# A contiguous copy of each position's spectrum ahead of its matmuls, and one pipeline of four stages for all rows

## The chip, the cores and the metric

The kernel runs on one core of one Trainium2 chip. The metric is the time of one execution in device microseconds, as the median of several runs. All data is float32 (or float32r, a one-pass float32 matmul form, where the code says F32R).

## What is computed

A gate mixes two branches over the same input `x` (2048 tokens, 640 features):

```python
def _A_ref(x, wqkv, wo):          # 32 heads of 20, each token sees itself and 7 others, 2 apart
    ...
    logits = jnp.einsum("bhsd,bhswd->bhsw", q, kg) * scale
    ...
    attn = _softmax(logits, axis=-1)
    o = jnp.einsum("bhsw,bhswd->bhsd", attn, vg)
    return (lambda x, *d: x.transpose(*d))(o, 0, 2, 1, 3).reshape(B, S, D) @ wo

def _B_ref(x, w_r, w_i):          # a filter in the two-dimensional spectrum
    X = jnp.fft.rfft2(x, axes=(-2, -1))
    X = X * (w_r + 1j * w_i)
    return jnp.fft.irfft2(X, s=(S, D), axes=(-2, -1))

x = A_x
g = _sigmoid((x * gate_w).sum(-1, keepdims=True))
return g * _A_ref(x, A_wqkv, A_wo) + (1 - g) * _B_ref(x, B_w_r, B_w_i)
```

## The kernel before, in words

**Tiling.** Token number 16p + j stands in partition p at position j, so there are 128 partitions and `NJ` = 16 positions. The transform over the 2048 tokens is one of length 128 over the partitions (matmuls with the table `fc`) followed by a step of length 16 over the positions. The spectrum lies in one SBUF tile `zg` of shape [128, 5, 16, 8, 16]: the partition is one of 128 feature frequencies, then come 5 chunks t of feature frequencies, 16 groups g of row frequencies, 8 entries c of a group, and last the position j. For a fixed chunk and group, the 128 numbers (c, j) lie side by side. For a fixed chunk and position, the 128 numbers (g, c) lie 16 numbers, 64 bytes, apart.

**Stages.** (1) `qkv`: the projection in three F32R matmuls per product (high and low halves), written to DRAM and read back by `attend`, which runs 16 units of attention mostly on DVE and POOL. (2) `cols`: the transform over the partitions, written by ACT into `zg` with a step of 64 bytes (`zg<-z`). (3) `freq(g)` (lines 919 to 1021), for 16 groups: matmuls with `zg[:, t, g]` as the stationary operand (`u`, `v`), the step over positions, the filter on DVE and POOL, and the way back over features of the group, copied by ACT into `zg` again (`zg<-g`, two copies for a group, chunks 0 to 2 and 3 to 4). (4) `project_even(j)`: the output projection for even positions, ending in a transfer to DRAM (`ad`). (5) `spatial(j)` (lines 1039 to 1109), the way back over rows for one position: six matmuls with the 128 numbers `zg[:, t, :, :, j]` as the stationary operand give `oa` and `ob`; ACT copies them to `os`; four matmuls with `fct` give `ha` and `hb`; for an odd position ACT scales these to `ho` and stops there, for an even one ACT and DVE make the row `y` (six DVE instructions, `h`, `ha`, `y`) and POOL adds it to what `project_even` left, by a transfer that accumulates (`yi<-y`, positions 0 to 8) or an addition. (6) `project_odd(j)` (lines 1140 to 1174): POOL folds `ho` into `ye` and `y`, PE projects the odd positions (`oTp`, `woa`, `wob`), DVE adds.

A matmul in float32 stands in the trace as two instructions, each with its own load of weights (PEld); one in F32R stands as one.

**Order.** `Plan` records every operation, with the buffers it reads and writes, and a planner (lines 286 to 481) then decides the order on each engine from its own costs and a seeded search over 250 variations; each engine runs its list strictly in that order. All instructions therefore carry line 666, and the tile names tell them apart. A buffer that two names share (a tag of a ring) must be used in the order in which the program names its users. `staged(gens, n)` names the steps of several generators so that n of them are under way at once.

**Tags and banks that matter here.** `oa` and `ob` turn over PSUM banks 0 to 2, `ha` over 3 and 4, `hb` has 5; `project_odd` takes banks 0 to 4 in turn for `woa`, `wob`, so the `wob` of its second position stands in bank 3. `ev0` and `ev1` hold the tables `mm` of `freq` until its last group; `x6` holds products of `freq` (line 573) and then `ye` of `project_odd` (line 577). The rows `y` turn over `raw3`, `raw4`, `e0` and `ya` (line 578).

Of the kernel before, what the change touches and what calls it, by code (L numbers as in the profile page):

```python
# [17 lines left out]
NJ = 16  # L18
# [487 lines left out]
def staged(gens, n):  # L506
    for step in range(len(gens) + n - 1):
        for i in range(max(0, step - n + 1), min(step, len(gens) - 1) + 1):
            next(gens[i], None)


class Ring:
# [5 lines left out]
    def next(self, name, *shape, dtype=F32):  # L518
        self.turn += 1
        tag = self.tags[(self.turn - 1) % len(self.tags)]  # L520
        return self.pool.tile([128, *shape], dtype, tag=tag, name=name, bufs=1)


class Mixer:
# [17 lines left out]
    def places(self, pp, dr, sb):  # L542
        self.pp, self.sb = pp, sb
        qb = self.pp.tile([128, 512], F32, tag="qbank", name="qbank")
        self.qthird = [qb[:, GC * i : GC * i + GC] for i in range(3)]
        self.qturn = -1
        self.qkv_d = dr.tile([8, 6, ROWS, HC], F32, tag="dram_qkv", name="qkvd")
        self.o_d = [dr.tile([128, 8, D], F32, tag=f"dram_o{i}", name=f"od{i}") for i in range(2)]
        self.f_d = dr.tile([128, 8, 2, D], F32, tag="dram_f", name="fd")
        self.a_d = dr.tile([128, 8, D], F32, tag="dram_a", name="ad")  # L550
        self.ident, self.fc = (self.one(n, 128) for n in ("ident", "fc"))
        self.fct = self.one("fct", 2, 128)
        self.z, self.g, self.ng, self.nng = (self.one(n, NJ) for n in ("z", "g", "ng", "nng"))
        make_identity(self.nc, self.ident)
        self.low = self.one("low", 64)
        self.nc.gpsimd.memset(self.low, -1e9)

        def ring(*tags):
            return Ring(sb, *tags)

        def n(tag, k):
            return ring(*(f"{tag}{i}" for i in range(k)))


        self.kvr, self.Lr, self.qr, self.prr = n("kv", 6), n("L", 3), n("q", 2), n("pr", 2)
        self.mr, self.sr, self.orr, self.pvr = n("m", 2), n("s", 2), n("o", 2), n("pv", 2)

        self.xr, self.wr, self.evr, self.rawr, self.fr = n("x", 8), ring(*WPLACES), n("ev", 2), n("raw", 5), n("f", 2)
        self.er, self.xor = ring("fe0", "fe1"), ring("raw0", "raw1", "raw2", "raw3", "raw4", "kv4", "kv5", "ya")

        self.vsr, self.mdr, self.mfr, self.wpr = n("raw", 2), n("ev", 2), ring("mf"), n("f", 2)
        self.abr, self.Pr, self.s12r, self.Xr = ring("x0", "x1"), ring("x2", "x3"), ring("x4", "x5"), ring("raw3", "raw4")
        self.p1r = ring("x6", "raw2")

        self.wor, self.war, self.yar = ring("ya", "w7"), ring("w2", "w3", "w4", "w0", "w1", "w5", "w6"), ring("ya")
        self.otr, self.oTr = (ring("w7"), ring("w7", "kv2")), (ring("x7"), ring("x7", "pr0"))
        self.osr, self.hor, self.hyr, self.yer = n("raw", 3), n("x", 4), ring("x4", "x5"), ring("x6")
        self.yr, self.yir = ring("raw3", "raw4", "e0", "ya"), n("f", 2)
        self.banks = {}
# [9 lines left out]
    def work(self):  # L589
        p, ins = self.p, self.ins  # L590
        S = p.sp
        self.xT, self.wh, self.wl, self.folded = {}, {}, {}, {}
        self.xraw, self.wraw = {}, {}
        self.warm()
        xe = self.one("xe", 8, 2, 5, 128, dtype=F32R, tag="big")
        st = [t[:, i] for t in (self.xr.next(f"st{i}", 2, 641) for i in range(7)) for i in range(2)]
        p.rank = 1e6
        self.load_x(st, xe[:, 0], 0)
        self.load_w(st, 0)
        for j in range(2, NJ, 2):  # L600
            self.load_x(st, xe[:, j // 2], j)
        self.xr.turn = 0
        self.fold(0)
        self.fold(1)
        rank, p.rank = p.rank, 0.0
        S.dma_start(self.fc, ins["t_fc"][:, 0:128])
        self.zero_rows()
        self.qkv(0, 0)
        p.rank = rank
        for j in range(1, NJ, 2):  # L610
            self.load_x(None, self.xr.next(f"xo{j}", 2, 5, 128, dtype=F32R), j)
        p.rank = 0.0
        for q in STORED:
            self.fold(q)
        self.qkv(1, 0)
        for hg in (1, 2, 3):
            self.load_w(None, hg)
            self.qkv(0, hg)
            if hg == 1:
                self.qkv(1, hg)  # L620
        self.zg = self.one("zg", 5, 16, 8, NJ, tag="big")
        todo = list(range(8))

        def columns(jj):
            if jj % 2:
                q = todo.pop(0)
                self.cols(q)
                if q + 2 in STORED:
                    self.load_f(q + 2)
                elif q < 6:  # L630
                    self.fold(q + 2)

        self.qkv(1, 2, columns)
        self.qkv(1, 3, columns)
        self.bt, self.gt = self.one("bt", 1288, tag="e0"), self.one("gt", 1288, tag="e1")
        S.dma_start(self.bt[:, 0:1284], ins["t_bt"])
        S.dma_start(self.gt, ins["t_gt"])
        S.dma_start(self.fct.rearrange("p v m -> p (v m)"), ins["t_fc"][:, 128:384])
        self.gates()
        self.load_wo()  # L640
        for u in UNITS[:-2]:
            staged([self.attend(*u)], 3)
        pair = [self.attend(*u, 2) for u in UNITS[-2:]]
        for _ in range(5):
            for a in pair:
                next(a, None)
        p.chain = ""
        freq = [self.freq(g) for g in GORD]
        staged(freq, 4)
        p.chain = "even"  # L650
        for j in range(0, NJ, 2):
            self.project_even(j)
        p.chain = ""
        staged([self.spatial(j) for j in range(1, NJ, 2)], 2)
        staged([self.spatial(j) for j in range(0, NJ, 2)], 3)
        odd = [self.project_odd(j) for j in range(1, NJ, 2)]
        next(odd[0])
        for this, later in zip(odd, odd[1:] + [iter(())]):
            next(later, None)
            next(this, None)  # L660
# [378 lines left out]
    def spatial(self, j):  # L1039
        p = self.p  # L1040
        V, A, T = p.dve, p.act, p.pe
        zg, gt = self.zg, self.gt
        o1, o2 = (self.ps((0, 1, 2), f"o{i}{j}") for i in "ab")

        def mm(o, t, r, start, stop):
            T.matmul(o, zg[:, t, :, :, j].rearrange("p g c -> p (g c)"), r, start=start, stop=stop, skip_group_check=True)

        mm(o1[:, 0:322], 1, gt[:, 161:483], True, False)
        mm(o1[:, 0:161], 0, gt[:, 0:161], False, False)
        mm(o1[:, 161:322], 2, gt[:, 483:644], False, True)  # L1050
        mm(o2[:, 0:322], 3, gt[:, 805:1127], True, False)
        mm(o2[:, 0:161], 2, gt[:, 644:805], False, False)
# [7 lines left out]
        for i, h in enumerate((h1, h2)):  # L1060
            for a in range(2):
# [4 lines left out]
                    start=(a == 0),  # L1066
                    stop=(a == 1),
                    skip_group_check=True,
# [182 lines left out]
```

## Time and profile before

| | |
|---|---|
| median of 3 runs (lowest, highest) | 465.19 us (464.69, 466.1) |
| the profiled execution: its own time, and the span of its trace | 464.31 us, 462.5 us |
| granted TensorE clock in it | 0.999 |
| busy shares over the span | PE 98%, PEld 87%, DVE 85%, ACT 48%, POOL 73% |

PE is a matmul, PEld a load of weights, which can run beside a matmul; DVE, ACT and POOL are the vector, scalar and GpSimd engines, SP issues most transfers. A row of instructions gives start, duration, engine, line, operation, `out<-in`, and in brackets the idle time just ahead of it with what ended that time. The ends of matmuls are modelled, so a busy PE is not PE at its peak. In this trace `freq` ends, and `spatial` begins, near 340 us; the last `ha` of `spatial` starts near 418 us, and what follows is `project_odd`.

### The profile page before, as it was taken

Reading aid. Unit: us, or ns where it says so; the run is one execution under the profiler, and the core shown is the slowest. Engines: PE = TensorE matmul, PEld = TensorE weight load, DVE = VectorE, ACT = ScalarE, POOL = GpSimd, SP = SyncE. Lnnn points to the kernel's source line nnn. Section 1 sums busy time; section 2 is a strip of 40 time slices with the busy share of each in tenths; the row PEclk is TensorE's granted clock in tenths of the full one; section 3 lists DMA queues with packets and bytes.
Section 4 is the critical chain, followed back from the end, with each engine's and each line's share of the span. In section 5 each row is a group of like instructions: output and inputs, shape, how many; then the busy total and the mean of one; then the engine's idle time right before and its main releaser. Section 6 shows DMA issues by size and latency. Waiting matters only on the chain.

```text
span 462.5 us, 7087 instructions
## 1 busy us (share of the span) xinstructions
PE 454.7 (98%) x2437; PEld 404.6 (87%) x2437; DVE 394.9 (85%) x515; ACT 221.2 (48%) x546; POOL 339.9 (73%) x296
## 2 busy tenths in 40 slices
PE   8999999999999999999999999999999999999996
PEld 5888888888888889898888878988889999999996
DVE  4545799999999999999999989999997897969443
ACT  5464364233332234565578587676745444332110
POOL 1075066879999998997599997355867966856796
PEclk9999999999999999999999999999999999999999
DMA  8995989585657749899797758866433132676842
GB/s 303 373 312 161 374 256 350 165 244 154 206 158 224 220 119 330 260 308 285 211 356 218 216 194 229 289 213 187 142 101 95 44 96 73 178 208 177 250 171 85
DMA packets 87283, 98.65 MB, mean 213 GB/s; under 512 B 20416, under 2 KB 74816, under 8 KB 87248
## 3 DMA queue, kind: packets, MB, share of 16 engines
q1 hardware_dynamic: 47616, 63.64, 43.9%
q10 hardware_dynamic: 38864, 32.86, 22.6%
q0 software_dynamic: 768, 1.71, 2.0%
q8 instruction: 19, 0.31, 0.3%
q14 instruction: 16, 0.13, 0.1%
HBM read 66.33 MB, written 30.22 MB: 209 GB/s over the span
## 4 chain that ended last, share of the span: by engine, by line
PE 78%; issue 7%; DVE 5%; DMA 5%; POOL 3%; ACT 2%; ACTq 0%; POOLq 0%; DVEq 0%
PE qkv L666 33%; PE woa L666 7%; PE wob L666 6%; PE oa L666 5%; PE ob L666 5%; PE z L666 4%; PE v L666 3%; PE g L666 3%; PE u L666 3%; PE hb L666 2%; PE ha L666 2%; DMA xt<-in_xT 2%; PE oTp L666 2%; POOL xo L666 2%; PE xa L666 2%
## 5 line engine op out<-in xcount | busy, mean ns | idle before, releaser
L666 PE MATMUL qkv<-w,xo 128*128 128x480 f32 (+1 forms) x480 | 114.0, 386 | 0.0
L666 PE MATMUL qkv<-w,xe 128*128 128x480 f32 (+1 forms) x465 | 105.4, 382 | 0.2 <-POOL w L666 0.2
L666 PEld LDWEIGHTS qkv<-w,xo 128*128 128x128 f32 x480 | 89.4, 189 | 13.4
L666 PEld LDWEIGHTS qkv<-w,xe 128*128 128x128 f32 x465 | 87.5, 189 | 15.4 <-POOL w L666 0.6
L666 ACT COPY ev<-qkv 128x480 f32<-128x480 f32 x64 | 35.7, 559 | 50.1 <-PE qkv L666 38.8
L666 PE MATMUL woa<-wo,oT 128*128 128x320 f32 x240 | 49.2, 316 | 0.1
L666 PE MATMUL wob<-wo,oT 128*128 128x320 f32 x240 | 48.4, 313 | 0.0
L666 PEld LDWEIGHTS woa<-wo,oT 128*128 128x128 f32 x240 | 38.4, 188 | 0.7 <-ACT oT L666 0.3
L666 PEld LDWEIGHTS wob<-wo,oT 128*128 128x128 f32 x240 | 38.5, 188 | 0.0
L666 POOL TENSOR_TENSOR P<-X,wp 128x642 f32<-128x642 f32 x16 | 24.9, 1556 | 18.3 <-ACT X L666 17.3
L666 POOL TENSOR_TENSOR w<-raw,w 128x480 fp32r<-128x480 f32 x15 | 18.2, 1239 | 19.5 <-ACT w L666 19.5
L666 POOL TENSOR_TENSOR xo<-xt,xo 128x640 fp32r<-128x640 f32 x8 | 12.4, 1580 | 22.2 <-ACT xo L666 20.0
L666 PE MATMUL oa<-gt,zg 128*128 128x161 f32 (+1 forms) x96 | 28.0, 408 | 0.6 <-ACT zg L666 0.6
L666 ACT CAST oT<-oTp 128x384 fp32r<-128x384 f32 (+1 forms) x32 | 13.0, 427 | 28.6 <-PE oTp L666 23.8
L666 PE MATMUL ob<-gt,zg 128*128 128x161 f32 (+1 forms) x96 | 26.6, 402 | 0.0
L666 DVE TENSOR_TENSOR oT<-oTp,oT 128x384 fp32r<-128x384 f32 (+1 forms) x32 | 15.0, 485 | 12.9 <-ACT oT L666 12.9
L666 PEld LDWEIGHTS g<-mm,s 128*128 128x128 f32 x150 | 20.9, 191 | 4.3 <-ACT zg L666 2.0
L666 PEld LDWEIGHTS oa<-gt,zg 128*128 128x128 f32 x96 | 23.8, 305 | 0.8 <-ACT zg L666 0.8
L666 PEld LDWEIGHTS ob<-gt,zg 128*128 128x128 f32 x96 | 24.1, 305 | 0.0
L666 ACT COPY zg<-z 128x512 f32<-128x512 f32 (+1 forms) x24 | 20.7, 948 | 6.4 <-PE z L666 6.4
L666 PE MATMUL g<-mm,s 128*128 128x128 f32 x150 | 22.8, 277 | 0.3 <-ACT zg L666 0.3
L666 PE MATMUL u<-bt,zg 128*128 128x321 f32 (+2 forms) x96 | 22.4, 345 | 0.0
(304 smaller groups left out, 1087.5 us busy)
## 6 DMA issues: line engine op xcount, KB each, us to landing
qkvd<-ev ACTq DMA_DIRECT2D x32, 480.0 KB, 4.1
wp<-in_ws SPq DMA_DIRECT2D x16, 642.0 KB, 4.6
fx<-in_x SPq DMA_DIRECT2D x8, 648.0 KB, 7.8
ot<-od SPq DMA_DIRECT2D x16, 320.0 KB, 3.6
raw<-in_wqkv SPq DMA_DIRECT2D x15, 240.0 KB, 5.6
xt<-in_xT SPq DMA_DIRECT2D x8, 320.0 KB, 8.7
ad<-ya SPq DMA_DIRECT2D x8, 320.0 KB, 4.7
yi<-ad SPq DMA_DIRECT2D x8, 320.0 KB, 3.3
```

The costliest lines, as they stand in the source:

```text
L666: p.dve.memset(w, 0.0)
```

## The change

Each position first gets a contiguous copy `zj` of its 640 numbers, made by ACT from `zg`, in one of three buffers (`ev0`, `ev1`, `x6`) in turn. The six matmuls take their weights from the copy. The copy is a stage of its own (a `yield` follows it), and the two pipelines, odd positions two deep and then even ones three deep, become one, four deep, with the odd positions first.

```diff
+        self.zjr = ring("ev0", "ev1", "x6")
...
-        staged([self.spatial(j) for j in range(1, NJ, 2)], 2)
-        staged([self.spatial(j) for j in range(0, NJ, 2)], 3)
+        staged([self.spatial(j) for j in [*range(1, NJ, 2), *range(0, NJ, 2)]], 4)
...
+        zj = self.zjr.next(f"zj{j}", 5, 128)
+        A.copy(zj, zg[:, :, :, :, j].rearrange("p t g c -> p t (g c)"))
+        yield
         o1, o2 = (self.ps((0, 1, 2), f"o{i}{j}") for i in "ab")
 
         def mm(o, t, r, start, stop):
-            T.matmul(o, zg[:, t, :, :, j].rearrange("p g c -> p (g c)"), r, start=start, stop=stop, skip_group_check=True)
+            T.matmul(o, zj[:, t], r, start=start, stop=stop, skip_group_check=True)
```

The planner makes a new order for the whole program. Three places show it. The numbers behind the names tell uses of one tile apart and differ by a few between the two kernels.

The first place is PE where `freq` ends and `spatial` begins. `g_0_810` and `g_3_811` are the two halves of the last group's way back over features, `oa`, `ob` the first position. Before:

```order
L666 MATMUL g_0_810<-mm_761,s_809 128x128 x3
L666 MATMUL oa_868<-gt,zg 128x322
L666 MATMUL oa_868<-gt,zg 128x161 x2
L666 MATMUL g_3_811<-mm_761,s_809 128x128 x2
L666 MATMUL oa_874<-gt,zg 128x322
L666 MATMUL ha_871<-os_870,fct 128x161
```

And now on PE:

```order
L666 MATMUL g_3_811<-mm_761,s_809 128x128 x2
L666 MATMUL oTp_849<-ident,ot_847 128x128 x3
L666 MATMUL ob_870<-gt,zj_868 128x322
L666 MATMUL oa_869<-gt,zj_868 128x322
L666 MATMUL oa_869<-gt,zj_868 128x161
L666 MATMUL ob_870<-gt,zj_868 128x161
```

and on ACT at the same place:

```order
L666 ACTIVATE ya_844<-wob_846,g 128x320
L666 COPY zg<-g_3_811 128x2x128
L666 COPY zj_868<-zg 128x640
L666 COPY zj_872<-zg 128x640
L666 CAST oT_848<-oTp_849 128x384
L666 COPY zj_879<-zg 128x640
L666 COPY os_871<-oa_869 128x2x161
L666 COPY os_871<-ob_870 128x2x161
L666 COPY os_878<-oa_876 128x2x161
L666 CAST oT_848<-oTp_850 128x256
L666 COPY zj_885<-zg 128x640
L666 ACTIVATE ho_875<-hb_874,ng 128x322
```

Before, `oa` of the first position needed chunks 0 to 2 only and stood ahead of `g_3`. Now the first copy needs all chunks, so it stands behind `zg<-g_3`, and between `g_3` and the first `ob` PE has only three `oTp`.

The second place is POOL in the last units of attention (`pv7a`, `pv7b` are products for DVE's sums, `yi` rows of even positions, `ye` the folding of odd ones). Before:

```order
L666 DMA yi_942<-y_946 128x640
L666 TENSOR_TENSOR pv7b_576<-vt7b,L7b 128x8x80 x2
L666 TENSOR_TENSOR pv7a_578<-vt7a,L7a 128x8x80 x2
L666 TENSOR_TENSOR pv7b_580<-vt7b,L7b 128x8x80 x2
L666 DMA yi_950<-y_954 128x640
```

And now:

```order
L666 TENSOR_TENSOR pv7b_576<-vt7b,L7b 128x8x80 x2
L666 TENSOR_TENSOR ye_992<-ho_875 128x2x161
L666 DMA yi_955<-y_960 128x640
L666 TENSOR_TENSOR ye_992<-ho_875 128x160 x2
L666 TENSOR_TENSOR pv7a_578<-vt7a,L7a 128x8x80 x2
L666 TENSOR_TENSOR pv7b_580<-vt7b,L7b 128x8x80
L666 DMA yi_964<-y_969 128x640
```

`ye_992` is written into `x6`, whose last copy, `zj_968` of position 12, is read by PE until near the end of `spatial`. It now stands ahead of the transfer `yi_955` and of the last products of attention; before, the first `ye` came early, among the products of the unit before.

The third place is DVE at the end of the even positions (`y_991` and `y_986` are positions 14 and 12, from `ha_987` and `ha_979`; `oT` belongs to the first odd projections). Before it read:

```order
L666 SCALAR_TENSOR_TENSOR h_965<-ha_963,ng,h_965 128x161
L666 SCALAR_TENSOR_TENSOR h_965<-ha_963,nng,h_965 128x160
L666 SCALAR_TENSOR_TENSOR ha_963<-ha_963,ng,h_965 128x160
L666 SCALAR_TENSOR_TENSOR ha_963<-ha_963,ng,h_965 128x161
L666 TENSOR_TENSOR y_970<-ha_963,h_965 128x321
L666 TENSOR_TENSOR y_970<-ha_963,h_965 128x319
```

And now:

```order
L666 TENSOR_TENSOR y_991<-ha_987,h_989 128x321
L666 TENSOR_TENSOR y_991<-ha_987,h_989 128x319
L666 SCALAR_TENSOR_TENSOR h_981<-ha_979,ng,h_981 128x161
L666 TENSOR_TENSOR oT_1001<-oTp_1003,oT_1001 128x256
L666 SCALAR_TENSOR_TENSOR h_981<-ha_979,nng,h_981 128x160
L666 SCALAR_TENSOR_TENSOR ha_979<-ha_979,ng,h_981 128x160
L666 TENSOR_TENSOR oT_1001<-oTp_1002,oT_1001 128x384
L666 SCALAR_TENSOR_TENSOR ha_979<-ha_979,ng,h_981 128x161
L666 TENSOR_TENSOR y_986<-ha_979,h_981 128x321
L666 TENSOR_TENSOR y_986<-ha_979,h_981 128x319
```

In both, the bank of position 12 (`ha_963`, now `ha_979`) is the one that `wob` of the second odd position takes next (`wob_997`, now `wob_1013`), so that matmul waits for the last of these rows.

## The prediction

> **What bounds the kernel now.** I read the page first: which engine is full, and on whom the chain that ended last runs.
>
> ```profile
> PE 454.7 (98%) x2437; PEld 404.6 (87%) x2437; DVE 394.9 (85%) x515; ACT 221.2 (48%) x546; POOL 339.9 (73%) x296
> PE 78%; issue 7%; DVE 5%; DMA 5%; POOL 3%; ACT 2%; ACTq 0%; POOLq 0%; DVEq 0%
> ```
>
> PE is full and carries the chain; DVE comes next. The change touches one stage, so I then asked for the windows of that stage, of the stretch inside it in which the even positions run, and of the stage behind it. Columns: length, then busy time of PE, PEld, DVE, ACT, POOL.
>
> ```profile
> 339.57:417.67 78.10, 78.10 (x421) 77.13 (x421) 65.43 (x85) 33.06 (x84) 55.74 (x48) 1.00 0.40 110
> 385.46:425.70 40.24, 40.11 (x229) 39.26 (x228) 33.00 (x65) 14.47 (x33) 28.45 (x25) 1.00 0.60 161
> 417.67:459.00 41.33, 41.19 (x288) 40.37 (x286) 23.27 (x46) 6.69 (x17) 33.61 (x45) 1.00 0.60 183
> ```
>
> In `spatial` PE is never idle for 78.1 us, PEld is nearly as full (77.1), and ACT has more than half its time free. So a microsecond that PE saves there is one that the end can move, as long as the others keep up. Whether there is one to save is told by the groups by shape, weight loads first:
>
> ```profile
> L666 PEld LDWEIGHTS ob<-gt,zg 128*128 128x128 f32 x96 | 24.1, 305 | 0.0
> L666 PEld LDWEIGHTS oa<-gt,zg 128*128 128x128 f32 x96 | 23.8, 305 | 0.8 <-ACT zg L666 0.8
> L666 PEld LDWEIGHTS v<-bt,zg 128*128 128x128 f32 x96 | 15.7, 190 | 3.2
> L666 PE MATMUL oa<-gt,zg 128*128 128x161 f32 x64 | 16.5, 372 | 0.0
> L666 PE MATMUL v<-bt,zg 128*128 128x161 f32 x32 | 7.0, 299 | 0.0
> ```
>
> `v` and `oa` load 128 columns from the same tile, `v` side by side and `oa` 64 bytes apart: 190 ns against 305 ns. The matmul of 161 columns lasts 372 ns with the second and 299 ns with the first. What a whole group of three matmuls (six instructions) takes when it runs undisturbed stands in the chain, which gives start and length:
>
> ```profile
> 242.52 1.09 PE u L666 x6
> 243.60 1.09 PE v L666 x6
> 366.41 1.42 PE ob L666 x6
> 370.75 1.41 PE ob L666 x6
> ```
>
> The shapes are alike (321, 161 and 160 columns; 322, 161 and 161): 1.09 us from contiguous weights, 1.41 us from strided ones.
>
> **The change, part by part. The weights.** There are 192 instructions `oa` and `ob` (twice x96 above), 32 groups of six. Each group falls from 1.41 to 1.09 us: 32 x 0.32 = 10.2 us less of PE. Nothing else covers those loads, since PE is busy throughout, so I count all of it. The matmul rows give 73 ns for a 161, which for the 128 of that shape is 9.3 us before the 322s, so 9.3 to 11.7 us is the span of this term (11.7 if the 64 of 322 gain half as much).
>
> [...]
>
> **The copies.** ACT gets 16 copies of 640 numbers, read 64 bytes apart. No row reads so. The nearest ones:
>
> ```profile
> L666 ACT COPY zg<-z 128x512 f32<-128x512 f32 x16 | 17.0, 1092 | 6.4 <-PE z L666 6.4
> L666 ACT COPY zg<-z 128x256 f32<-128x256 f32 x8 | 5.3, 660 | 0.0
> L666 ACT CAST xe<-st 128x640 fp32r<-128x640 f32 x7 | 4.9, 733 | 0.1
> ```
>
> `zg<-z` writes with that step: 1092 - 660 = 432 ns for 256 numbers, 1.69 ns each, so 1092 + 128 x 1.69 = 1.31 us for 640. The contiguous cast of 640 takes 0.73 us, the lower end. I take 1.31, since its pattern is the same with reading and writing swapped, and allow 2.0 above. ACT's work in the stage becomes 33.1 + 16 x 1.31 = 54 us, against 78.1 - 10.2 = 67.9 us of PE: it fits, and from the second position on the copies are made ahead. The first ones are not:
>
> ```profile
> 338.16 0.84 PE L666 MATMUL g<-mm,s 128*128 128x128 f32 x6
> 339.57 1.70 PE L666 MATMUL oa<-gt,zg 128*128 128x322 f32 x6 [0.57 <-ACT zg L666]
> L666 ACT COPY zg<-g 128x256 f32<-128x256 f32 x16 | 6.0, 373 | 0.9 <-PE g L666 0.7
> 337.77 0.55 PE L666 MATMUL oTp<-ident,ot 128*128 128x128 f32 x3 [0.17 <-ACT ya L666]
> ```
>
> Before, PE waits 0.57 us here. Now the last `g` is followed on ACT by `zg<-g` (0.37) and the copy (1.31), 1.68 us, with some 0.1 for the `ya_844` ahead of them; PE meanwhile has three `oTp`, about 0.35 us. So it waits 1.4 us, 0.85 more than before. The next copies come in time (1.31 us each, while PE spends 2.18 on the first position), but `zj_885` stands in ACT's queue ahead of `os_878<-ob_877`, for which `hb` waits: by adding up the list, some 0.4 us. Together 1.3 us, from 0.3 (copy at 0.73) to 2.7 (at 2.0).
>
> [...]
>
> **The turn to the odd projections.** The faster PE asks more of DVE. These rows are the first DVE instruction on an even position, those on the last one (one of them left out), the PE matmul that takes over its bank, the window between, and a line of the waits:
>
> ```profile
> 386.22 0.39 DVE L666 SCALAR_TENSOR_TENSOR h<-ha,ng,h 128x161 f32<-128x161 f32 x1 [1.02 <-ACT h L666]
> 423.05 0.37 DVE L666 SCALAR_TENSOR_TENSOR h<-ha,ng,h 128x161 f32<-128x161 f32 x1
> 423.75 0.82 DVE L666 SCALAR_TENSOR_TENSOR ha<-ha,ng,h 128x160 f32<-128x160 f32 x2
> 424.61 0.89 DVE L666 TENSOR_TENSOR y<-ha,h 128x321 f32<-128x321 f32 x2
> 425.70 0.31 PE L666 MATMUL wob<-wo,oT 128*128 128x320 f32 x1
> 386.22:425.54 39.32, 39.19 (x224) 38.34 (x223) 32.84 (x65) 13.78 (x32) 27.69 (x24) 1.00 0.61 163
> DVE h L666 <- PE ha L666: 3.3, 1, 3.3
> ```
>
> DVE ended at 425.50 and `wob` began at 425.70: the two were just in step. From the first `ha` of the even positions (385.46) to there PE took 40.24 us. In the new order the same stretch holds 12 of the 322s, 27 of the 161s, 32 `ha` and `hb`, 62 `wo` and 15 `oTp`. A 322 is half a group, 0.545 us, a 161 0.27; the chain gives 0.27 to a `ha` or `hb`, 2.21 to 15 `wo` and 0.55 to 5 `oTp`:
>
> ```profile
> 363.82 0.27 PE ha L666 x2
> 456.79 2.21 PE wob L666 x15
> 449.64 0.55 PE oTp L666 x5
> ```
>
> That is 6.5 + 7.4 + 8.8 + 9.1 + 1.7 = 33.5 us. DVE has the same eight reductions, 48 row instructions and six `oT` there, 32.8 us of work. Of its 6.5 us of idle time 3.3 were a wait for PE, which goes; the other 3.2, mostly for ACT, I leave. It starts 0.76 us after the `ha`: 0.8 + 32.8 + 3.2 = 36.8, so `wob_1013` waits 3.3 us if nothing moves closer together. A part of those 3.2 us should be lost in the crowding, and I take 2.5, from 0 to 5.
>
> **The wait through `x6`** ends at the same matmul. POOL holds `ye_992` until the last `ob_975`, and behind it in POOL's queue stand `yi_955` and the last products of attention. `y_991` needs the buffer that `yi_955` reads.
>
> ```profile
> L666 POOL TENSOR_TENSOR ye<-ho 128x322 f32<-128x322 f32 x8 | 6.1, 757 | 0.5
> yi<-y POOLq DMA_DIRECT2D x5, 320.0 KB, 5.0
> L666 POOL DMA_DIRECT2D yi<-y x5 | 4.7, 935 | 2.8 <-DVE y L666 2.8
> ```
>
> From the end of `ob_975` to `wob_1013` PE has 9.6 us in the new order (32 `wo`, 8 `ha` and `hb`, 10 `oTp`, half a position). The chain is 0.76 (`ye`) + 0.94 + 5.0 (transfer) and then on DVE 0.9 (`y_991`) + 2.45 (the row `y_986`, as 423.05 to 425.50 above) + about 0.9 (two `oT`) = 11.0 us: late by 1.4, inside the 2.5 already charged. If that were the later one with a transfer 2 us slower, it would be 3.4. The products behind `ye_992` feed position 13, some 25 us further on, and cost nothing.
>
> **The rest of the order** is new as well. Before `spatial` the engines keep the same instructions, and the same five even projections stand ahead of it on PE; I charge nothing and allow 2 us either way, about what PE idles ahead of `spatial`, most of it here (busy time of PE second, 0.67 and 0.94 us short):
>
> ```profile
> 300.00:320.00 20.00, 19.33 (x117) 16.20 (x116) 18.50 (x32) 15.07 (x40) 9.42 (x8) 1.00 0.76 227
> 320.00:340.00 20.00, 19.06 (x122) 17.00 (x122) 19.04 (x33) 13.45 (x35) 18.45 (x15) 1.00 0.43 129
> ```
>
> **The sum** against the profiled execution (464.31 us; its span is 462.5, the 1.8 around it stays): -10.2 + 1.3 + 2.5 = -6.4, so 457.9 us. That execution lies 0.9 under the median of 465.19, so for the median 458.8 us.
>
> **The rivals.** (a) *Nothing is paid back.* DVE closes up and the first copies are nearer 0.73 us: -10.2 + 0.3, with up to 1.5 us more saved on the 322s: 453.8 to 455.3 us. For it speaks that before, DVE had 6.5 us idle in the even stretch; against it that its work there alone is 32.8 us in PE's 33.5.
>
> (b) *DVE or the chain through `x6` becomes the bound of the even positions* and takes most of the gain: turn 5 us, first copies 2.7, 1 to 2 us elsewhere: 463.7 to 464.7 us, near no change. For it: DVE at 65.4 of 78.1 us, which against 67.9 would be 96%.
>
> (c) *ACT becomes the bound, and the kernel slower.* Its place is ACT's queue in `spatial`, where the copies stand ahead of the `os` that free the banks. ACT's own 33.1 us and 16 copies fill PE's 67.9 us from 2.2 us a copy, and the 78.1 us of before from 2.8 us. At 3.0 us the stage takes 33.1 + 48 = 81.1 us, with the first two copies in the open (1.7 us later each than in the sum): 465.2 + 3.0 + 3.4 = 471.6 us. Against it: the slowest row of that pattern would have to be more than doubled.
>
> (d) *The change doesn't do what it says*: the load costs what its columns cost, and the 372 ns had another cause, such as the tables or the neighbours. Then PE saves nothing and only the first copies are paid: 465.2 + 1.3 = 466.5 us. [...] Against it stand 96 loads at 190 ns beside 192 at 305 in one trace.
>
> **How the numbers follow.** A measurement here can tell about 0.3%, 1.4 us, from no change: 463.8 to 466.6 us. My forecast, 456 to 462 us, gets 0.58, (a) 0.15, (b) 0.15, (c) 0.06, (d) 0.06. All of the forecast and (a) and 0.09 of (b) are faster: 0.82; the rest of (b) and half of (d) are the same: 0.09; (c) and half of (d), where the new order loses a little on top, slower: 0.09. The range runs from 454.0, the full gain, to 464.0 us, into (b); what lies outside is (c), (d), part of (b) and a full gain with a better order.
>
> **What would show it.** `oa` and `ob` read `zj` with loads near 190 ns and groups of 1.09 us; the stage from the first `ob` to the last `ha` near 69 us, not 78; copies of about 1.3 us; PE idle about 1.4 us ahead of the first `ob`; a wait of PE for DVE of some 2.5 us near the second odd position; the odd stage as long as before. I am wrong if the loads stay at 305 ns, if copies take 2 us or more, if PE waits for `os` again and again in the stage, or if the loss lies ahead of 340 us.

## The result, and the profile after

The changed kernel takes 457.58 us (median of 4 runs, 456.91 to 459.44), the kernel before 465.46 us (median of 4, 464.69 to 466.1): a ratio of 0.9838, 95% interval 0.9805 to 0.9871, or 7.9 us less. The forecast was 458.8 us within 454.0 to 464.0. The profiled execution took 456.91 us, with a span of 455.1 us against 462.5.

Two lines of the page after, the busy times and the chain that ended last:

```profile
PE 443.6 (97%) x2437; PEld 388.8 (85%) x2437; DVE 393.8 (87%) x515; ACT 238.8 (52%) x562; POOL 339.9 (75%) x296
PE 78%; DMA 7%; DVE 6%; ACT 3%; issue 3%; POOL 2%; POOLq 0%; SPq 0%; ACTq 0%; DVEq 0%
```

PE's busy time fell from 454.7 to 443.6 us, 11.1 us, yet the span only by 7.4: so 3.7 us of new idle time on PE have to be found. ACT gained 17.6 us, DVE and POOL did the same work as before. The groups by shape show where the 11.1 us come from (busy time, then mean ns of one):

```profile
L666 PEld LDWEIGHTS ob<-gt,zj 128*128 128x128 f32 x96 | 15.6, 190 | 3.1 <-ACT zj L666 1.3
L666 PEld LDWEIGHTS oa<-gt,zj 128*128 128x128 f32 x96 | 15.3, 189 | 1.1
L666 PE MATMUL oa<-gt,zj 128*128 128x161 f32 x64 | 12.3, 299 | 0.0
L666 PE MATMUL oa<-gt,zj 128*128 128x322 f32 x32 | 11.3, 434 | 0.0
L666 ACT COPY zj<-zg 128x640 f32<-128x640 f32 x16 | 21.1, 1330 | 0.0
```

The loads went from 305 to 190 ns, the matmul of 161 columns from 372 to 299 ns, that of 322 from 479 to 434; its row before was

```profile
L666 PE MATMUL oa<-gt,zg 128*128 128x322 f32 x32 | 12.7, 479 | 0.6 <-ACT zg L666 0.6
```

A copy takes 1.33 us. An undisturbed group of six, from the chain:

```profile
346.07 1.09 PE oa L666 x6
```

The windows of the stage from its first `ob` to just short of its last `ha`, and of the stage behind it:

```profile
343.62:411.20 67.58, 67.58 (x425) 62.01 (x426) 62.85 (x84) 50.12 (x101) 54.59 (x46) 1.00 0.45 118
411.20:451.00 39.80, 39.45 (x277) 38.95 (x276) 22.17 (x44) 5.88 (x15) 33.69 (x45) 1.00 0.65 204
```

The stage itself shrank from 78.1 to 67.6 us and PE is never idle in it (the two windows do not hold quite the same instructions, 421 and 425). But it begins at 343.62 us, not at 339.57. Part of that is order (before, 1.4 us of `oa` stood ahead of the last `g`); the rest is lost in two places. The first is just ahead of the stage, on PE and on ACT:

```profile
341.24 0.60 PE L666 MATMUL g<-mm,s 128*128 128x128 f32 x4
342.02 0.55 PE L666 MATMUL oTp<-ident,ot 128*128 128x128 f32 x3 [0.18 <-ACT ya L666]
343.62 0.81 PE L666 MATMUL ob<-gt,zj 128*128 128x322 f32 x2 [1.05 <-ACT zj L666]
```

```profile
341.44 0.53 ACT L666 ACTIVATE ya<-wob,g 128x320 f32<-128x320 f32 x1 [1.74 <-PE wob L666]
341.88 0.37 ACT L666 COPY zg<-g 128x256 f32<-128x256 f32 x1
342.29 2.48 ACT L666 COPY zj<-zg 128x640 f32<-128x640 f32 x2
```

PE stands 1.05 us for the first copy, where it stood 0.57 us before. The second place lies far ahead, in stages that the change does not touch. The same windows of the kernel before, then of the changed one:

```profile
0.00:10.00 10.00, 8.00 (x24) 4.87 (x24) 4.14 (x8) 5.27 (x8) 2.04 (x9) 1.00 0.82 286
40.00:80.00 40.00, 39.82 (x183) 34.05 (x182) 31.77 (x31) 17.79 (x57) 15.30 (x14) 1.00 0.94 309
sum 340.00, PE 335.81 PEld 287.57 DVE 306.06 ACT 181.44 POOL 250.96; mean PE 30.53 PEld 26.14 DVE 27.82 ACT 16.49 POOL 22.81
```

```profile
0.00:10.00 10.00, 7.54 (x21) 4.64 (x22) 3.33 (x7) 4.54 (x7) 2.04 (x9) 1.00 0.81 280
40.00:80.00 40.00, 38.80 (x178) 33.05 (x177) 33.15 (x31) 17.08 (x53) 19.66 (x18) 1.00 0.89 296
sum 340.00, PE 333.65 PEld 285.58 DVE 304.16 ACT 180.70 POOL 248.40; mean PE 30.33 PEld 25.96 DVE 27.65 ACT 16.43 POOL 22.58
```

In the first 340 us PE does 2.2 us less work than before. Of its 4.2 us of idle time there before, 0.74 us belong to the seam (0.17 and 0.57); the 6.35 us of now all lie ahead of it. So 2.9 us of new idle time lie ahead of the seam, 0.5 at it and 0.2 behind the stage, together nearly the 3.7. The planner searches one order for the whole program, so a change in its last fifth gave the first four fifths a new one, in which PE waits once for 1.2 us for ACT's `ev`. Two single executions can't tell how much of the 2.9 us is the order; the first experiment times it.

### The profile page after: what moved, and what is told of

Same layout as the page of the kernel before. It is cut to its first block, busy times and chain, and to the rows that moved or that the text cites. A ratio compares the mean times of both kernels' runs of the same rounds, so it can differ in the third digit from the quotient of the medians.

```text
span 455.1 us, 7098 instructions
## 1 busy us (share of the span) xinstructions
PE 443.6 (97%) x2437; PEld 388.8 (85%) x2437; DVE 393.8 (87%) x515; ACT 238.8 (52%) x562; POOL 339.9 (75%) x296
## 4 chain that ended last, share of the span: by engine, by line
PE 78%; DMA 7%; DVE 6%; ACT 3%; issue 3%; POOL 2%; POOLq 0%; SPq 0%; ACTq 0%; DVEq 0%
PE qkv L666 37%; PE wob L666 6%; PE woa L666 6%; PE z L666 4%; PE ob L666 4%; PE oa L666 4%; PE v L666 3%; PE g L666 2%; PE u L666 2%; DMA raw<-in_wqkv 2%; PE hb L666 2%; PE ha L666 2%; DMA xt<-in_xT 2%; PE xa L666 2%; PE oTp L666 2%
## 5 line engine op out<-in xcount | busy, mean ns | idle before, releaser
L666 PE MATMUL qkv<-w,xo 128*128 128x480 f32 (+1 forms) x480 | 115.7, 385 | 1.2 <-ACT ev L666 1.2
L666 PE MATMUL woa<-wo,oT 128*128 128x320 f32 x240 | 46.7, 319 | 0.0
L666 PE MATMUL wob<-wo,oT 128*128 128x320 f32 x240 | 46.3, 317 | 0.4 <-ACT oT L666 0.4
L666 PE MATMUL ob<-gt,zj 128*128 128x161 f32 (+1 forms) x96 | 22.1, 345 | 1.1 <-ACT zj L666 1.1
L666 PE MATMUL oa<-gt,zj 128*128 128x161 f32 (+1 forms) x96 | 23.1, 344 | 0.0
L666 PE MATMUL v<-bt,zg 128*128 128x321 f32 (+2 forms) x96 | 21.8, 346 | 0.1
L666 ACT COPY zj<-zg 128x640 f32<-128x640 f32 x16 | 21.1, 1330 | 0.0
L666 PEld LDWEIGHTS v<-bt,zg 128*128 128x128 f32 x96 | 15.8, 190 | 4.0 <-ACT vs L666 0.6
```

The costliest lines, as they stand in the source:

```text
L666: p.dve.memset(w, 0.0)
```

## The experiments

My theory: the 64-byte step of the weights cost about 11 us and the copies take it away; the change gives some back through the first copy and the new order. The main rival: the single pipeline with its new order is the gain and the weights come along. Several kernels keep an order fixed to the instruction, so that only the named operand or copy differs.

**The changed kernel, weights from `zg` again, order untouched.** The copies are made and nobody reads them:

```
 def mm(o, t, r, start, stop):
     T.matmul(o, zj[:, t], r, ...)
+    p.ops[-1].call[1]["a"] = (o, zg[:, t, :, :, j].rearrange("p g c -> p (g c)"), r)
```

> The changed kernel in its own order, instruction for instruction, but every oa and ob takes its weights from zg at the 64-byte step; the sixteen copies are still made and nobody reads them. Theory (the step of the weights is the gain): loads back at 305 ns, groups at 1.41 us, PE busy 11.1 us more, less about 1.0 us because PE no longer waits for the first copy: 457.6 + 11.1 - 1.0 = 467.7 us, between 466 and 469, that is 2 us over the kernel before, which is what the new order would then cost. Rival (the single pipeline and its new order are the gain, the weights come along): 456 to 459 us.

Measured: 467.17 us (5 runs), ratio to the kernel before 1.0037 (1.0017 to 1.0056). One row of its groups and one of its chain:

```profile
L666 PEld LDWEIGHTS oa<-gt,zg 128*128 128x128 f32 x96 | 24.3, 306 | 0.1
```

```profile
346.26 1.42 PE oa L666 x6
```

With the strided weights the whole gain is gone. What is left, 1.9 us more than before (0.8 to 2.6 by the interval), is the price of the new order, with the unread copies still on ACT. PE waits for no copy here and has shed the 0.57 us of before as well, so the order costs some 2.5 us (1.4 to 3.2).

**The kernel before, contiguous weights, no copies, order untouched:**

```
-    T.matmul(o, zg[:, t, :, :, j].rearrange("p g c -> p (g c)"), r, ...)
+    T.matmul(o, zg[:, t, j].rearrange("p c i -> p (c i)"), r, ...)
```

> The kernel before in its own order, without any copy, but oa and ob take as weights 128 neighbouring numbers of the same tile (the block of one group of frequencies), so the numbers that come out are not the rows of the reference; shapes and count of instructions stay. Theory: loads 190 ns, groups 1.09 us, PE saves the full 11.1 us: 465.5 - 11.1 = 454.4 us, 453 to 457, the upper end if DVE holds PE up at the turn to the odd projections. It is then 2 to 4 us under the changed kernel, and that distance is what copies and new order cost. Rival (pipeline and order are the gain): 464 to 466 us.

Measured: 454.43 us (4 runs), ratio 0.9764 (0.9745 to 0.9783), 10.8 us less than the 465.23 us of the kernel before beside it.

```profile
L666 PEld LDWEIGHTS oa<-gt,zg 128*128 128x128 f32 x96 | 15.2, 189 | 1.1
```

```profile
PE oTp L666 <- DVE oT L666: 1.1, 2, 0.8
```

This is the weight term by itself, in the old order and with the old pipelines. Between it and the changed kernel lie 3.15 us. Even here, by the line of its waits, DVE holds PE up at most 1.1 us in two places.

**One half of the change each.** First the single pipeline without copies (`staged(..., 3)` over all rows, weights from `zg`):

> The kernel before with one half of the change alone: all rows in one pipeline (three stages, since there is no copy stage), weights from zg at the 64-byte step, planned anew. Theory (weights are the gain): none of it here, 465.5 us with 2 us either way from the new order. Rival (the single pipeline has a gain of its own): 463 us or less.

Measured: 465.14 us (10 runs), ratio 1.0000 (0.9987 to 1.0012). Then the copies with the two pipelines of before (`staged` of the odd rows with 3, of the even rows with 4):

> The changed kernel with the copies but the two pipelines of before (odd rows in three stages, then even rows in four), planned anew. Theory (weights are the gain, the pipeline does nothing): 457.6 us with 2 us either way from the new order. Rival (the single pipeline has a gain of its own): 460 us or more.

Measured: 456.01 us (4 runs), ratio 0.9807 (0.9785 to 0.9829). The pipeline alone gives nothing, the copies alone give it all. The new order of the first of the two costs nothing either, so the 2.5 us are the price of one order, not of any new one. That it lies 1.6 us under the changed kernel is no sign against the single pipeline: the intervals overlap, and it has a searched order of its own.

**Two buffers instead of three** (`ring("ev0", "ev1")`, planned anew):

> The changed kernel with two buffers for the copies, without x6, planned anew. Theory (from the second position on the copies are made well ahead, and x6 holds nobody up): no loss in the stage, 457.6 us with 2 us either way from the new order. Rival (three buffers are needed: a copy can start only when PE has left the position before last, and PE then waits for it): 0.4 us at each of 14 positions, 463 us. Second rival (x6 holds POOL's ye back and POOL's late finish sets the end): 1 to 2 us faster, with POOL done sooner.

Measured: 458.51 us (4 runs), ratio 0.9860 (0.9829 to 0.9891). No loss and no gain can be told beside the changed kernel's interval, with a new order of its own; the rival's 463 us are ruled out. Neither the third buffer nor the chain through `x6` decides anything of that size.

**Each copy made twice**, order untouched:

```
 A.copy(zj, zg[:, :, :, :, j].rearrange("p t g c -> p t (g c)"))
+once = p.ops[-1].call[1]["fn"]
+p.ops[-1].call[1]["fn"] = lambda *a: (once(*a), once(*a))
```

> The changed kernel in its own order with each of the sixteen copies made twice over, so that ACT spends 2.66 us on a position. Theory of a limit (from about 2.2 us a copy ACT's queue sets the stage): ACT's 50.1 us in the stage become 71.4 us against PE's 67.6: 3.8 us longer, and 1.3 us more ahead of the first ob: 457.6 + 5.1 = 462.7 us; by the figure of the prediction (33.1 + 42.6 = 75.7 us) it would be 467. Rival (ACT has room to the end, only the first copy lies open): 457.6 + 1.3 = 458.9 us.

Measured: 469.58 us (4 runs), ratio 1.0089 (1.0071 to 1.0108): slower than without the change. The window of its stage (the columns as above), and PE's stops in it with the copies' own row:

```profile
345.10:422.73 77.63, 70.62 (x426) 62.23 (x427) 61.69 (x82) 67.74 (x116) 54.33 (x45) 1.00 0.38 102
```

```profile
L1046 ACT COPY zj<-zg 128x640 f32<-128x640 f32 x32 | 41.9, 1316 | 0.5
```

```profile
345.10 0.81 PE L666 MATMUL ob<-gt,zj 128*128 128x322 f32 x2 [2.37 <-ACT zj L1046]
350.88 0.54 PE L666 MATMUL hb<-os,fct 128*128 128x161 f32 x2 [1.67 <-ACT os L666]
379.50 0.54 PE L666 MATMUL hb<-os,fct 128*128 128x161 f32 x2 [1.01 <-ACT ho L666]
387.84 2.46 PE L666 MATMUL wob<-wo,oT 128*128 128x320 f32 x15 [1.65 <-ACT ya L666]
```

At 2.6 us for each position the stage takes 77.6 us instead of 67.6, more than either of my sums. ACT is not even full: 67.7 us of 77.6. Apart from the first, no stop is a wait for a copy. PE waits for `os`, `ho` and `ya`, short reads of banks (0.43 us for `os`, 0.53 for `ho` and `ya`) that stand in ACT's queue behind two or four copies in a row. So here the order of ACT's queue sets the pace while the engine is idle for 13% of the stage.

**The old order ahead of the stage, the new one from there on.** A table gives the first 2644 operations of the kernel before their old places:

```
-order = self.order()
+order = sorted(self.order(), key=lambda op: PLACE.get(op.i, 1 << 30))
```

> The changed kernel, with every instruction ahead of the way back over rows put in the order of the kernel before (2644 operations, up to its first oa) and everything from there on in the order of the changed kernel. Theory (the 2 us lost ahead of the stage come from the newly searched order alone): 457.6 - 2.0 = 455.6 us, 454.8 to 456.6, with no PE wait of 1.2 us for ev and 0.7 us left over the kernel with contiguous weights and no copies (454.4), which is the wait for the first copy. Rival (the copies themselves cost the 3 us, in the stage and behind it): 457 to 458 us.

Measured: 457.97 us (5 runs, 455.52 to 458.44), ratio 0.9823 (0.9799 to 0.9846). By the median the theory fails and the rival holds; the single executions, sorted by their clock only after the times were seen, say more. Two, at a mean clock of 1.000, took 455.52 and 455.96 us, as the theory has it; three, at 0.995 to 0.996, took 457.97 to 458.44. One of the latter was profiled. On PE, and in windows (the third column from the end is the granted clock):

```profile
340.77 0.71 PE L666 MATMUL g<-mm,s 128*128 128x128 f32 x4 [0.57 <-ACT zg L666]
343.26 1.13 PE L666 MATMUL ob<-gt,zj 128*128 128x322 f32 x2 [1.77 <-ACT zj L666]
```

```profile
341.00:343.00 2.00, 0.49 (x4) 0.29 (x3) 1.97 (x3) 1.45 (x2) 0.98 (x2) 1.00 0.84 286
343.40:343.80 0.40, 0.40 (x2) 0.31 (x3) 0.40 (x1) 0.40 (x1) 0.00 (x0) 0.77 0.10 38
344.20:346.40 2.20, 2.20 (x8) 1.80 (x7) 2.20 (x3) 1.38 (x2) 0.86 (x1) 0.50 0.00 0
346.80:347.20 0.40, 0.40 (x4) 0.40 (x3) 0.40 (x1) 0.09 (x1) 0.40 (x2) 0.71 0.61 152
```

The seam has made the wait for the first copy longer, 1.77 us, with 0.57 us of idling shortly before it. From about 343.6 to 347.0 us the clock stands at 0.50: 3.4 us, when the stage has hardly begun. A pair of 161s starts every 0.54 us there (345.79, 346.33, 346.87), against 0.27 in the changed kernel (345.09, 345.36, 345.63); by that half of the 3.4 us, an estimated 1.7, is lost. That asked for a test of its own, in both directions.

**The same kernel with less idle time there** (the first two positions read `zg` and have no copy; the first `oa` stands ahead of the last `g` again):

> The kernel of the run with the old head, in its order, but the first two positions are read from zg at the 64-byte step and have no copy, and the first oa stands ahead of the last g again, as in the kernel before. PE then has no wait for a copy ahead of it: it idles 0.6 us there instead of 2.3 us, and 12 of the 192 matmuls stay slow (2 x 0.64 = 1.3 us). Theory (the wait for the first copy costs its own length, and in some executions lets TensorE's granted clock fall to 0.5 for 3.4 us besides, worth 2 us or more): no drop of the clock in any execution, times in one cluster, 454.4 + 1.3 = 455.7 us, 455 to 456.5. Rival (the drop comes by chance and has nothing to do with the wait): again some executions near 458 us with a mean clock of 0.996, the median between 456 and 458.

Measured: 456.80 us (5 runs, 455.49 to 458.26), ratio 0.9818 (0.9793 to 0.9843). PE's longest wait there is 0.57 us. The mean clock is 0.999 or 1.000 in all five executions, as the theory has it. The times are not: the median lies outside the 455 to 456.5 us expected, and they are no single cluster, with 2.8 us of spread at full clock, whose cause stays open.

**And with more** (the first copy alone made twice):

> The kernel of the run with the old head, in its order, with the first copy alone made twice over, so that PE waits 1.3 us longer ahead of the first ob: 3.1 instead of 1.8 us. Theory (the drop of the clock follows PE's idle time): every execution has the drop, mean clock 0.996 or less, 455.7 + 1.3 + 2.3 = 459.3 us in one cluster. Rival (the drop comes by chance): two clusters as before, 457.0 and 459.3 us, about as often as in the run with the old head (3 of 5).

Measured: 459.27 us (4 runs, 459.06 to 460.21), ratio 0.9878 (0.9863 to 0.9894). All four executions have a mean clock of 0.993 to 0.996, as the theory has it. The profiled one, at 0.993, stands at 0.50 from about 342.6 to 349.4 us, 6.8 us, and the drop begins while PE still waits:

```profile
344.19 1.44 PE L666 MATMUL ob<-gt,zj 128*128 128x322 f32 x2 [3.09 <-ACT zj L1047]
```

```profile
342.00:343.00 1.00, 0.00 (x0) 0.00 (x0) 1.00 (x2) 0.97 (x2) 0.00 (x0) 0.80 0.56 213
343.00:344.00 1.00, 0.00 (x0) 0.00 (x0) 1.00 (x2) 1.00 (x1) 0.00 (x0) 0.50 0.06 23
348.00:349.00 1.00, 1.00 (x5) 0.99 (x4) 0.34 (x1) 0.54 (x2) 1.00 (x2) 0.50 0.00 0
349.00:350.00 1.00, 1.00 (x6) 0.73 (x4) 0.00 (x0) 0.32 (x1) 1.00 (x2) 0.78 0.00 0
```

Over all kernels whose matmuls read copies, by PE's wait ahead of its first `oa` or `ob` in the profiled execution:

| wait (us) | kernels | executions with a mean clock under 0.997 |
|---|---|---|
| 0.6 to 1.1 | first two direct, changed kernel, two pipelines | 0 of 13 |
| 1.8 | two buffers, old head | 5 of 9 |
| 2.4 | each copy twice | 2 of 4 |
| 3.1 | first copy twice | 4 of 4 |

Only two of these eleven low clocks were profiled (old head and first copy twice); that the other nine lie at the same place is not shown. The profiled executions of the kernels with two buffers and with each copy twice waited 1.8 and 2.4 us and kept the full clock.

**How much step is too much.** Two kernels in the order of before, `oa` and `ob` each at a step of their own (`flat[:, at : at + 128 * step : step]`):

> The kernel before in its own order, with the weights of oa read at a step of 8 bytes and those of ob at 16 bytes (other numbers of the same tile, so the output is not the reference's; contiguous is 4 bytes, the kernel before 64). It asks what of the 115 ns between 190 and 305 hangs on the step. Theory A (the load slows in proportion to the span read): 198 ns for oa, 213 for ob. Theory B (any step costs the whole): 305 ns for both, and the time of before. Theory C (only some step or more costs): 190 ns for one or both.

> As the run with steps of 8 and 16 bytes, with oa at 32 bytes and ob at 128 bytes; again with other numbers of the tile. Theory A: 244 ns for oa and 428 for ob. Theory B: 305 ns for both. Theory C: 190 or 305 ns for oa, 305 for ob.

Measured once each: 458.71 us and 464.85 us, beside 465.0 us of the kernel before. The groups of the first kernel, then of the second:

```profile
L666 PEld LDWEIGHTS oa<-gt,zg 128*128 128x128 f32 x96 | 15.5, 196 | 1.0
L666 PEld LDWEIGHTS ob<-gt,zg 128*128 128x128 f32 x96 | 25.0, 319 | 0.2
```

```profile
L666 PEld LDWEIGHTS oa<-gt,zg 128*128 128x128 f32 x96 | 25.4, 327 | 0.0
L666 PEld LDWEIGHTS ob<-gt,zg 128*128 128x128 f32 x96 | 24.2, 307 | 0.0
```

4 bytes cost 190 ns, 8 bytes 196, 16 bytes 319, 32 bytes 327, 64 bytes 305, 128 bytes 307. For the steps tried it is a threshold between 8 and 16 bytes (theory C), not a slope.

## Why the prediction was right, and where only by luck

**Weights (forecast -10.2 us).** Right in kind, a little small: -10.8 us by the kernel with contiguous weights, -11.1 us of PE's busy time. A group fell from 1.41 to 1.09 us as said, and both figures lie within the 9.3 to 11.7 given. With that rival (d), "the load costs what its columns cost", is out: 128 columns take 190 ns at one step and 305 ns at another. Nor do all loads at the contiguous step take 190 ns: the shortest of 128 columns by their mean are those of `oTp`, 140 ns; why stays open:

```profile
L666 PEld LDWEIGHTS oTp<-ident,ot 128*128 128x128 f32 x80 | 10.1, 140 | 2.0 <-DVE oT L666 0.8 <-ACT ya L666 0.6
```

**Copies (1.31 us each, +1.3 in all).** A copy takes 1.33 us; the row of the mirrored pattern was the right one to take, not the contiguous 0.73. In the open lies less than charged: PE idles 1.23 us there in two pieces (0.18 and 1.05) instead of 1.4, 0.5 more than the 0.74 of before (0.17 and 0.57), since the three `oTp` between cover 0.55 us, as the prediction's own row has it, and not 0.35. The second stop, 0.4 us for `os_878`, does not appear: two copies follow each other in 2.48 us, and PE has no idle time in the stage.

**The turn to the odd projections (+2.5).** This step failed, and not in size alone. The prediction let `wob_1013` wait for the row `y_986` of position 12, and the text on the change says that `wob` of the second odd position takes that position's bank. It does not. Counting through all users of that ring (the frequency stage takes 49 turns of it) gives position 12 bank 4 and position 14 bank 3; `wob_1013` and, before, `wob_997` take bank 3. So the matmul waits for `y_991`, in the changed kernel the earlier of these two DVE rows, and on PE the matmul in question:

```profile
414.34 0.89 DVE L666 TENSOR_TENSOR y<-ha,h 128x321 f32<-128x321 f32 x2
417.37 0.89 DVE L666 TENSOR_TENSOR y<-ha,h 128x321 f32<-128x321 f32 x2
```

```profile
412.16 0.56 PE L666 MATMUL wob<-wo,oT 128*128 128x320 f32 x2 [0.35 <-ACT oT L666]
417.49 0.31 PE L666 MATMUL wob<-wo,oT 128*128 128x320 f32 x1
```

It starts at 417.49, while DVE still writes the later row until 418.26, and 2.3 us after the earlier one ended (415.23). In the kernel before the distance was as large (`y_975` ended at 423.13, `wob` began at 425.70):

```profile
422.65 0.48 DVE L666 TENSOR_TENSOR y<-ha,h 128x319 f32<-128x319 f32 x1
```

"The two were just in step" was a coincidence of two times without a dependence behind it. The turn cost 0.35 us, and that is a wait for ACT. The estimate of PE's time there, 33.5 us, was good enough: it took 34.4 us from the earliest start of the first even `ha` (383.07 in the trace) to 417.49. So DVE was indeed close, but nobody stood behind it.

**The wait through `x6`** was rightly given no price of its own: without `x6` the time can't be told from the changed kernel's. Its working ended at the same wrong matmul, though.

**The rest of the order (0, allowed 2 either way).** This was the missing term: 2.5 us by the kernel with strided weights in the new order. Its reason, that ahead of the stage "the engines keep the same instructions", does not carry a zero: the same instructions came in another order there. Among its own signs of being wrong the prediction named a loss ahead of 340 us, and most of the loss lies there. The old order ahead of the stage agrees in the two executions at full clock (455.52 and 455.96 us), not by its median.

**The sum.** Forecast -10.2 + 1.3 + 2.5 + 0 = -6.4. Measured -10.8 + 0.5 + 2.5, the turn's 0.35 being part of the last, = -7.8, against -7.9 us between the medians. The forecast was near by luck: a charge for a wait that does not exist stood in for a loss that was not charged.

**The rivals.** (a), nothing paid back, is the kernel with contiguous weights, 454.4 us: a bound, not the outcome. (b) fell with the turn; its chance was also misread, since 0.09 of its 0.15 were counted as faster although of its 463.7 to 464.7 us only the first 0.1 lies under 463.8. (c) was the right danger in the right queue: at 2.66 us a copy it comes true, 469.6 us, where the prediction's own sum (33.1 + 16 x 2.66 = 75.7 us for the stage) was 2 us short of the 77.6 measured.

## What to carry to other kernels

Look at the mean time of a weight load for each layout before looking at the matmul: two tiles of one shape with two times (here 190 and 305 ns) point to the layout, which a kernel with contiguous weights in the same order settles. Here a copy of 1.33 us on an engine with room paid (457.58 us against 465.46), and made twice, with short reads held up behind it, it did not (469.58 against 465.23). Follow a wait to the exact buffer, through every user of its ring, before giving it a price; two times that agree are no dependence. When a planner orders the whole program, time the changed part with the order held fixed, or a gain of ten (here 10.8 us) and a random loss of two (2.5) look like a gain of eight (7.9).

## What was not expected of the hardware

**The threshold of the step.** A load of 128 fp32 weights took 190 ns at a step of 4 bytes, 196 at 8, and 305 to 327 at the four steps from 16 to 128 bytes. A step of two numbers is nearly free (196 ns), one of four is not (319 ns); what sets the threshold there is not shown.

**A short wait, and a lower clock.** With a wait of 1.8 us ahead of a full stage the mean clock lay under 0.997 in 5 of 9 executions, with 3.1 us in 4 of 4, with up to 1.1 us in none of 13; the two that were profiled show a granted clock of 0.50 for 3.4 us and for 6.8 us. Beside the wait itself this goes with 2 to 3 us in the kernels with two buffers and with the old head (460.43 and 459.42 against 457.43 and 457.6 us; 457.97 to 458.44 against 455.52 and 455.96). With each copy made twice no cost shows (469.76 and 468.37 us with a low clock, 469.41 and 469.92 without). The shortest wait after which a drop was profiled is 1.77 us, with 0.57 us of idling shortly before it; why the clock is low in only some executions of the kernels with 1.8 and 2.4 us is not shown.

**Left open:** the spread of 2 to 3 us at full clock (459.44 us in one execution of the changed kernel, 455.49 to 458.26 in five of the kernel with two direct positions). None of the variants that give the reference's output is faster than the changed kernel beyond the intervals, so no better version is claimed. A second tile, into which the frequency stage could write its result in the order that the loads want, was not tried; it would need another 40 KB in each partition (5 x 2048 numbers of 4 bytes).
